# Two streamed value steps ahead of the second half of a softmax, and the home of the last four value tiles, in a two-layer decode kernel

## The chip, the core and the metric

The kernel runs on one core of one Trainium2 chip. The metric is device time in microseconds (us) of one execution. The engines are named as the profile names them: PE (TensorE, matrix multiply; PEld is its loading of weights), DVE (VectorE), ACT (ScalarE), POOL (GpSimd) and SP (SyncE, which here issues nearly all transfers, in its program's order). SBUF is the on-chip memory, PSUM the memory in eight banks that PE accumulates into, HBM the memory off the core.

## The reference

The work is one decode step (one token for each of four batch elements) through four blocks in a row: attention, feed-forward, attention, feed-forward, with the same weights and the same key and value caches in both attentions.

```python
x = A_x                                   # 4 x 1 x 512
for _ in range(2):
    h = layernorm(x)
    q = h @ wq                            # 32 query heads of 128, 8 key/value heads
    s = q . k_cache / sqrt(128)           # 4096 positions a head, 4 query heads share one
    x = x + (softmax(s) @ v_cache) @ wo
    h = layernorm(x)
    x = x + (gelu(h @ w_gate) * (h @ w_up)) @ w_down     # 1792 wide
```

All arrays are bf16. The keys and values of one element are 16.8 MB; the whole kernel reads 102.5 MB from HBM. Nearly all of it is keys and values, a part of the values twice.

## The kernel before, in words

**Tiles.** A cache tile is half of one head's keys or values: 128 partitions x 16 positions x 128, 512 KB. An element has 16 key tiles and 16 value tiles, in two groups of four heads (`one(b)` lists the value tiles as pairs of head and half, the first group's eight and then the second's). Keys are loaded to `KP`, which holds one element's 16 key tiles; values go through a ring of eight slots, `v_t`.

**Rounds.** The keys of an element are loaded once for both attentions. So the second attention of element b - 1 and the first attention of element b are worked together: `attend(b)` (L920) takes the scores of the second layer of b - 1 while its keys are still there, loads and turns the keys of b in the same places, takes the scores of the first layer of b, and goes through values of both. I call attend(1), attend(2), attend(3) rounds 1, 2 and 3. `attend_first` (L847) comes before them and `attend_last` (L1029) after them. Behind each attend stands `dense` (L1080), the feed-forward layer of element b, and the query projection of its second layer.

**What is kept.** Of the 16 value tiles of an element the second layer takes the last three from the ring (`kept`), two from PSUM, where DVE copied them (`Parked`, L500, and ACT copies them back, L507), and eleven from HBM again: three `own` and eight `other`, the first group's (`two`, L586).

**Two ways through a value tile.** `vals1` and `vals2` (class Values, L711) step through tiles in order. Most heads are done by 16 matmuls with the value tile as weights (L759, tile `ot`). A *streamed* head has the probabilities as weights instead: `stream_v` (L687) does eight matmuls of 128x256 for a tile (L692, tile `so`), and `turn_v` and `sum_v` (L698 to L709) fold the sums: a transpose, a reduction and a scaling on DVE. The eight `other` tiles are left behind by attend(b) as `late2`, a `Streamed` (L794), and worked in the dense layer, in its PE gaps: `fill` is one step, `whole` folds the sums of a pair of heads. They stand: one step after the residual sum (L1113), one in the middle of the gate matmuls (L1118), two behind the up matmuls (L1109), the first fold (L1122), two behind the down matmuls (L1129), and two in the second layer's query projection (L1229, L1242) with the last fold (L1257).

**What sets the order.** Everything is written out by hand, engine by engine; no scheduler moves it. PE, DVE and ACT each go through their instructions in order and wait where data are missing. All loads of keys and values are issued by SP in the order of the program. For values that is the order of `ring.seq`, to which `ring.extend` adds, and `ring.pump` issues as many loads as there are free slots. A load waits on SP for its slot to be read, and with it all that stand behind it; a load also waits for the eighth one before it to land, since there are eight semaphores in turn. `pump_head` loads both halves of a head in one transfer of 1 MB to a place outside the ring.

In `attend` the ring's order is: the first layer's value tiles of b (14 of them; two are loaded ahead), the eight `other` tiles, three `own` (L959 to L961). After these come two first-layer tiles of the next element (L1240) and its keys. The keys can be loaded once the second layer's scores have been taken.

**Around the softmax.** The last softmax of a round is at L1003. `soft` (L525) reduces, transposes and reduces on DVE (L530, L534, L535), scales (L539) and has ACT take the exponentials (L542). `soft_turn` transposes on DVE (L550), `soft_swap` (L563) has PE lay out the probabilities (L572, tile `x`) and ACT copies them back (L575); `soft_den` and `soft_recip` give the denominators. PE does three value steps of the other group (L1004) while DVE and ACT do the softmax. Behind it come the eight value tiles of the second group with the output projection between them, and the last head's output `OL_bf` (L605).

**The last element.** Its eight `other` tiles find no next element. The query weights of group gx (`wq_sb[gx]`, four tiles' worth) are free once the last projection with them is done, so four tiles go there (L1236). The other four go to the key tiles of the first scores (L1042 to L1044), which are free when those scores have been taken. `dense_last` (L1132) is the last feed-forward layer, for all four elements at once.

Of the kernel before, what the change touches and what calls it, by code (L numbers as in the profile page):

```python
# [8 lines left out]
FP32 = mybir.dt.float32  # L9
# [6 lines left out]
P = 128  # L16
# [9 lines left out]
GH = 4  # L26
# [8 lines left out]
def kernel(  # L35
# [21 lines left out]
    KD = D // P  # L57
# [736 lines left out]
    class Streamed:  # L794
# [3 lines left out]
            self.b, self.tiles, self.prob, self.dst, self.n = b, tiles, prob, dst, 0  # L798
            self.sums = []

        def fill(self):
            kvh, t = self.tiles[self.n]
            self.n += 1
            g, s = divmod(kvh, GH)
            pe = self.prob[g][0]
            if t == 0 and s % 2 == 0:
                ps = ps_sc.tile([P, 2 * SW], FP32, name="so", tag="sc")
                self.sums.append((kvh, ps))
            ps = self.sums[-1][1]
            ring.pump()  # L810
            v, own = ring.ready.pop((2, self.b, kvh, t))
            at = s % 2 * SW
            stream_v(ps[:, at:at + SW], pe[:, s], v, t, t == 0, t == NT - 1)
            assert own
            ring.free.append(v)
            ring.pump()

        def whole(self):
            kvh, ps = self.sums.pop(0)
            g, s = divmod(kvh, GH)  # L820
            turn_v(ps, 2)
            sum_v(ps, self.dst(kvh, 2), self.prob[g][1][:, s:s + 2], 2)

    def dst1(b):
        last = one(b)[-1][0]
# [94 lines left out]
    def attend(b, qy, before, norm, early=None):  # L920
# [35 lines left out]
        for t in range(NT):  # L956
            scores(sc2[1], gy, t)
            keys.load(GH)
        ring.extend(1, b, one(b)[ahead_of[b]:])  # L959
        ring.extend(2, b - 1, other2)  # L960
        ring.extend(2, b, own1)  # L961
        pe0, den0 = soft_swap(p0, early=True), soft_den(p0)

# [38 lines left out]
        scores(sc1, gy, 1)  # L1002
        p0 = soft(sc1)  # L1003
        vals1.step(3)  # L1004
        soft_turn(p0)
        heads = pairs(one(b))
        twice = o1(b)
        rows = RowProj(lambda i: twice(i).broadcast_to([P, 2]))
        prob1[gy] = (soft_swap(p0), soft_recip(soft_den(p0)))
        vals1.step(2)  # L1010
        rows.heads(heads[0], hp)
        vals1.step(2)
# [16 lines left out]
    def attend_last(q_bf, norm):  # L1029
        b = B - 1  # L1030
        gx, gy = second_groups[b]
        prob2 = {}
        kept2, own2, other2, apart2 = two(b)
        tiles = kept2 + own2 + apart2 + other2
        vals = Values(2, b, tiles, prob2, dst2(b),
                      streamed=[h for h in range(Hkv) if h != tiles[-1][0]],
                      paired=[h for h in range(Hkv) if h // 2 != tiles[-1][0] // 2])
        banks.back()
        sc2 = [new_scores(early=True)]
        scores(sc2[0], gx, 0)  # L1040
        qe = q_sums(q_bf[:])
        ring.pump_head(KP[gx][0][0][:])  # L1042
        ring.pump([k_tile(gx * GH + 2, 0)])
        ring.pump([k_tile(gx * GH + 3, 0)])  # L1044
        scores(sc2[0], gx, 1)
        q_spread(qe)
        p0 = soft(sc2[0], norm)
        rows = RowProj(o2)
        sc2.append(new_scores())
        scores(sc2[1], gy, 0)  # L1050
        scores(sc2[1], gy, 1)
        soft_turn(p0)
        pe0, den0 = soft_swap(p0), soft_den(p0)
        p1 = soft(sc2[1], norm, lasting=True)
        prob2[gx] = (pe0, soft_recip(den0))
        vals.step(8, hold=True)
        soft_turn(p1)
        vals.flush()
        pe1, den1 = soft_swap(p1), soft_den(p1)
        prob2[gy] = (pe1, soft_recip(den1))  # L1060
        heads = pairs(tiles)
        full = ps_x.tile([P, KF, WIDE], FP32, name="gr", tag="x")
        nothing(full.rearrange("p c r -> p (c r)"))
        nc.scalar.preload_act_table_set("gelu_apprx_tanh_and_others")
        vals.step(4)
        rows.heads(heads[0], hp)
        rows.heads(heads[1], hp)
        vals.step(2)
        rows.heads(heads[2], hp)
        rows.split()  # L1070
        vals.step(2)
        proj = OutProj(o2, B)
        proj.heads(heads[3], rep)
        rows.onto(proj)
        proj.n = Hq - rep
        proj.heads(heads[3] + rep, rep)
        assert vals.left() == 0 and ring.at == len(ring.seq)
        return proj.y, full

    def dense(b0, nb, y, prev, scr):  # L1080
# [34 lines left out]
        add_y(b0, nb, y)  # L1115
        rstd, mr = ln_scale(nb, st)
        t = [None if first else shifts(scr, mr, i) for i in range(2)]
        g = out_of(0, into(wg_sb, "g", prev.fill))  # L1118
        sq = gelu(scr, g, shifts(scr, mr, 0) if first else t[0], rstd, up)
        uv = out_of(1, u[0]) if first else u[0]  # L1120
        H_bf = gate_up(scr, sq, uv, shifts(scr, mr, 1) if first else t[1], rstd)
# [3 lines left out]
            busy(1)  # L1125
            return y
        y = down_rows(H_bf)
        for _ in range(2):
            prev.fill()  # L1129
        return turn_rows(y)  # L1130

    def dense_last(y, full):  # L1132
# [66 lines left out]
        for k in range(KD):  # L1199
            (nc.sync, nc.scalar)[k % 2].dma_start(out=rows_out[:, k * P:(k + 1) * P],  # L1200
                                                  in_=xo[k * QS:k * QS + B, :])

    class NoValues:
        fill = whole = lambda self: None

# [4 lines left out]
    for b in range(B):  # L1210
# [14 lines left out]
        if b:  # L1225
# [5 lines left out]
                rest = q_rows(b, gy)  # L1231
            norm.root()
            if b == B - 1:
                last = two(b)[2]
                ring.extend(2, b, last[:KD])
                for t in range(0, KD, NT):  # L1236
                    ring.pump_head(wq_sb[gx][:, t:t + NT].rearrange("p t (c d) -> p t c d", d=Dh))
            q_build(q_bf[:])
            if b < B - 1:
                ring.extend(1, b + 1, one(b + 1)[:ahead_of[b + 1]])  # L1240
# [1 line left out]
            prev.fill()  # L1242
            if b == B - 1:
                banks.back_brief()
                ring.extend(2, b, last[KD:])
                q_bf = q_tile()
                q_round(q_bf, turn_rows(rest), gy, norm)
        else:
# [51 lines left out]
```

## Time and profile before

| | us |
|---|---|
| median of three runs | 273.52 |
| the three runs | 272.98, 273.52, 275.62 |
| the profiled execution | 273.24 |
| its span in the profile | 271.46 |
| PE busy, DVE busy, ACT busy | 180.9, 176.3, 54.1 |
| transfers of keys and values: share of the span that 16 DMA engines were busy with the queue | 94.8% |
| matmuls on the last value tile begin; the output's transfers are issued | 261.90; 268.76 |

The profile is of one execution, so times out of it are set against its own 273.24 us; 1.78 us of that lie around the span. Times in the text are us from the start of the span. A line of the chain or of the timeline has the start, the length, the engine, the tile written and the line in the program, and `x16` for sixteen instructions together; in brackets stands how long the engine idled before and what ended that. "SPq" is SP's queue and "DMA v_t" a transfer to a value slot from its issue to its landing. In the page's slices, each column is a fortieth of the span; PEclk is the granted clock of PE in tenths, DMA the busy share of the 16 DMA engines in tenths.

### The profile page before, as it was taken

The page shows a single profiled execution, that of the slowest core. Times are in us where ns is not written, and L with a number is a line of the kernel's source. Part 1 is how long each engine was busy: PE and PEld are TensorE (multiplying, and loading weights), DVE is VectorE, ACT ScalarE, POOL GpSimd, SP SyncE. Part 2 cuts the span into 40 slices and gives each one's busy share as a digit, 9 for nine tenths or more (in the row PEclk, how much of TensorE's full clock was granted, in tenths as well). Part 3 has the DMA queues.
Part 4 walks back from the last instruction along what each step waited for, and adds up shares of the span by engine and source line. Part 5 has one row for each costly group of instructions (what it writes and reads, how often), then busy time and mean ns, then how long its engine had stood idle before and what let it go on. Part 6 is the DMA issues. An engine that isn't in the chain of part 4 may idle for free.

```text
span 271.5 us, 8960 instructions
## 1 busy us (share of the span) xinstructions
PE 180.9 (67%) x3982; PEld 110.6 (41%) x3982; DVE 176.3 (65%) x445; ACT 54.1 (20%) x113; POOL 2.7 (1%) x8
## 2 busy tenths in 40 slices
PE   1366254644696956868669458787596596977784
PEld 1313133533363524445327134454262253543463
DVE  3394951131224898875776989667759894877673
ACT  1001001100005402031023520310226102105630
POOL 2000000000000000000000000000000000000001
PEclk9999999555599795779997977799978556799999
DMA  7999999999984999999999999999999999999930
GB/s 250 422 416 421 416 421 416 410 383 406 407 325 147 405 415 419 418 418 416 416 404 407 417 420 417 417 416 388 381 421 418 416 423 414 369 383 378 415 132 3
DMA packets 32286, 103.08 MB, mean 380 GB/s; under 512 B 2676, under 2 KB 8568, under 8 KB 32248
## 3 DMA queue, kind: packets, MB, share of 16 engines
q1 hardware_dynamic: 32224, 102.51, 94.8%
q8 instruction: 31, 0.51, 0.7%
q14 instruction: 7, 0.06, 0.0%
q10 hardware_dynamic: 24, 0.01, 0.0%
HBM read 102.50 MB, written 0.00 MB: 378 GB/s over the span
## 4 chain that ended last, share of the span: by engine, by line
DMA 37%; DVE 28%; PE 23%; SPq 6%; issue 3%; ACT 1%; DVEq 0%
DMA v_t<-in_A_v_cache_dram 18%; DVE kp L488 16%; PE sc L521 10%; DMA kp<-in_A_k_cache_dram 9%; DMA wd_sb<-in_B_w_down_dram 6%; DMA kp<-in_A_v_cache_dram 4%; SPq L143 4%; PE ot L759 3%; PE so L692 2%; DVE pe L530 2%; DVE qb L313 2%; PE y L248 2%; PE q L273 1%; DVE q L280 1%; SPq L144 1%
## 5 line engine op out<-in xcount | busy, mean ns | idle before, releaser
L488 DVE STREAM_TRANSPOSE kp<-kp 128x1024 f32<-128x1024 f32 x64 | 74.1, 1208 | 0.0
L521 PE MATMUL sc<-kp,qb 128*32 128x512 bf16 x512 | 57.9, 492 | 20.7 <-DVE kp L488 15.2
L759 PE MATMUL ot<-pe,v_t 128*128 128x32 bf16 x1120 | 34.9, 182 | 13.0 <-DMA v_t<-in_A_v_cache_dram 11.6
L759 PEld LDWEIGHTS <-v_t 128*128 128x128 bf16 x1120 | 33.2, 101 | 23.8 <-DMA v_t<-in_A_v_cache_dram 13.8
L521 PEld LDWEIGHTS <-qb 128*32 128x32 bf16 x512 | 17.0, 106 | 48.6 <-issue 34.6
L542 ACT ACTIVATE pe<-sc,nl 128x512 bf16<-128x512 f32 x8 | 5.5, 687 | 88.8 <-DVE pe L539 61.8
L572 PE MATMUL x<-pe,ident_bf 128*32 128x128 bf16 x192 | 6.3, 262 | 16.5 <-DVE pe L550 16.5
L530 DVE TENSOR_REDUCE pe<-sc 128x1 f32<-128x512 f32 x12 | 8.3, 690 | 11.8 <-PE sc L521 11.8
L572 PEld LDWEIGHTS <-ident_bf 128*32 128x32 bf16 x256 | 5.9, 109 | 19.5 <-issue 18.2
L692 PE MATMUL so<-v_t,pl 128*32 128x256 bf16 x192 | 9.5, 275 | 3.6 <-DMA v_t<-in_A_v_cache_dram 3.4
L248 PE MATMUL y<-OT_bf,wo_sb 128*128 128x32 bf16 x192 | 7.3, 190 | 6.9 <-DMA wo_sb<-in_A_wo_dram 6.7
L248 PEld LDWEIGHTS <-wo_sb 128*128 128x128 bf16 x256 | 8.5, 102 | 8.1 <-DMA wo_sb<-in_A_wo_dram 7.1
L700 DVE STREAM_TRANSPOSE so<-so 128x256 f32<-128x256 f32 (+1 forms) x19 | 11.1, 583 | 1.0 <-PE so L692 0.9
L692 PE MATMUL so<-v_t,pe 128*32 128x256 bf16 x208 | 10.6, 338 | 1.2 <-ACT pe L575 1.1
L507 ACT COPY v_t<-park 128x1024 bf16<-128x1024 bf16 x12 | 11.3, 1031 | 0.0
L550 DVE STREAM_TRANSPOSE pe<-pe 128x512 bf16<-128x512 bf16 x12 | 8.4, 698 | 4.4 <-ACT pe L542 4.4
L370 DVE TENSOR_TENSOR xb<-XX,y 128x4 bf16<-128x4 f32 (+1 forms) x9 | 1.6, 174 | 14.5 <-PE y L248 14.4
L575 ACT CAST pe<-x 128x512 bf16<-128x512 f32 x12 | 7.0, 586 | 19.0 <-PE x L572 19.0
L605 DVE TENSOR_TENSOR OT_bf<-ot,rden 128x8 bf16<-128x8 f32 (+1 forms) x20 | 3.1, 157 | 10.7 <-PE ot L759 10.5
L351 PE MATMUL yr<-wo_sb,OT_bf 128*2 128x512 bf16 (+1 forms) x96 | 9.8, 478 | 0.1
L248 PE MATMUL q<-xb,wq_sb 128*128 128x5 bf16 (+1 forms) x192 | 5.5, 170 | 6.5 <-DMA wq_sb<-in_A_wq_dram 6.5
L307 PE MATMUL qe<-q_bf,ident_bf 128*32 128x16 bf16 x256 | 4.4, 176 | 8.0 <-DVE q_bf L296 6.1
(142 smaller groups left out, 217.3 us busy)
## 6 DMA issues: line engine op xcount, KB each, us to landing
v_t<-in_A_v_cache_dram SPq DMA_DIRECT2D x97, 512.0 KB, 8.4
kp<-in_A_k_cache_dram SPq DMA_DIRECT2D x40, 512.0 KB, 12.1
kp<-in_A_k_cache_dram SPq DMA_DIRECT2D x12, 1024.0 KB, 7.4
wq_sb<-in_A_wq_dram SPq DMA_DIRECT2D x2, 2048.0 KB, 14.7
wo_sb<-in_A_wo_dram SPq DMA_DIRECT2D x4, 1024.0 KB, 11.6
wq_sb<-in_A_v_cache_dram SPq DMA_DIRECT2D x2, 1024.0 KB, 10.8
wg_sb<-in_B_w_gate_dram SPq DMA_DIRECT2D x1, 1792.0 KB
wu_sb<-in_B_w_up_dram SPq DMA_DIRECT2D x1, 1792.0 KB
```

The source lines that it names most:

```text
L143: dq.dma_start(out=wo_sb[:, i * n:(i + 1) * n], in_=wo_dram[:, i * n:(i + 1) * n])
L248: nc.tensor.matmul(dst, lhsT=lhsT, rhs=rhs, start=first, stop=last, skip_group_check=True)
L351: nc.tensor.matmul(self.rows[j:j + x.shape[1]], lhsT=x, rhs=wo_sb[:, i], start=self.n < QD, stop=True, skip_group_check=True)
L488: nc.vector.transpose(out=words, in_=words)
L507: nc.scalar.copy(out=dst[:, i * n:(i + 1) * n], in_=self.parts[i])
L521: nc.tensor.matmul(sc[s * QS:(s + 1) * QS], lhsT=qb[:, w0:w0 + 2 * W], rhs=kt[:, :, be // 2, :, be % 2], start=(t == 0 and be == 0), stop= ...
L530: nc.vector.tensor_reduce(out=m, in_=sc.rearrange("p c j -> p (c j)"), axis=AX.X, op=ALU.min if norm else ALU.max)
L550: nc.vector.transpose(out=flat, in_=flat)
L572: nc.tensor.matmul(x[a * QS:(a + 1) * QS, s], lhsT=ident_bf[:, s * QS:(s + 1) * QS], rhs=pT[:, a], start=True, stop=True, skip_group_check ...
L692: nc.tensor.matmul(ps[d, :NW * QS], lhsT=x[:, w:w + NW].rearrange("p c h -> p (c h)"), rhs=v[:, i:i + NW, d], start=first and i == 0, stop ...
L700: nc.vector.transpose(out=flat, in_=flat)
L759: nc.tensor.matmul(self.ot[:, s % 2], lhsT=v[:, i, :], rhs=wide(pe[:, s, t * CH + i, :]), start=(done == 0 and i == 0), stop=(done == NT - ...
```

## The change

It has two parts.

*Steps into the softmax wait.* Two of the eight `other` steps, both halves of the first head, leave the dense layer and stand behind the three value steps in the wait for the round's last softmax. Their sums go to a bank of their own (`ps_h`) and are folded right behind the layout matmuls of that softmax. The second head of the group now stands alone too, in a tile of one head's width, and the third and fourth are folded as a pair. In the dense layer there is no step in the middle of the gate matmuls any more and one instead of two behind the down matmuls; so the six steps there are: one after the residual sum, two behind the up matmuls, one behind the down matmuls, two in the query projection. The first of the pair's four steps is the second of the two behind the up matmuls; it writes the one bank of `ps_sc` in which the second head's sums still lie, and PE waits there only for its own earlier matmuls. The ring's order follows: the two tiles are loaded between the first group's and the second group's first-layer tiles. No load is added or left out.

*The last four tiles.* All eight `other` tiles of the last element go to the query weights' space: four to group gx's as before, and four to group gy's, in one transfer of 1 MB and two of 512 KB, which wait for the second projection (L1231) to have read it. The loads to the key tiles in `attend_last` are gone.

```diff
@@ -798,28 +798,30 @@
             self.b, self.tiles, self.prob, self.dst, self.n = b, tiles, prob, dst, 0
             self.sums = []
 
-        def fill(self):
+        def fill(self, early=False):
             kvh, t = self.tiles[self.n]
             self.n += 1
             g, s = divmod(kvh, GH)
             pe = self.prob[g][0]
-            if t == 0 and s % 2 == 0:
-                ps = ps_sc.tile([P, 2 * SW], FP32, name="so", tag="sc")
-                self.sums.append((kvh, ps))
-            ps = self.sums[-1][1]
+            alone = s < 2
+            if t == 0 and (alone or s % 2 == 0):
+                pool, tag = (ps_h, "h") if early else (ps_sc, "sc")
+                n = 1 if alone else 2
+                self.sums.append((kvh, n, pool.tile([P, n * SW], FP32, name="so", tag=tag)))
+            ps = self.sums[-1][2]
             ring.pump()
             v, own = ring.ready.pop((2, self.b, kvh, t))
-            at = s % 2 * SW
+            at = 0 if alone else s % 2 * SW
             stream_v(ps[:, at:at + SW], pe[:, s], v, t, t == 0, t == NT - 1)
             assert own
             ring.free.append(v)
             ring.pump()
 
         def whole(self):
-            kvh, ps = self.sums.pop(0)
+            kvh, n, ps = self.sums.pop(0)
             g, s = divmod(kvh, GH)
-            turn_v(ps, 2)
-            sum_v(ps, self.dst(kvh, 2), self.prob[g][1][:, s:s + 2], 2)
+            turn_v(ps, n)
+            sum_v(ps, self.dst(kvh, n), self.prob[g][1][:, s:s + n], n)
 
     def dst1(b):
         last = one(b)[-1][0]
@@ -956,8 +958,10 @@
         for t in range(NT):
             scores(sc2[1], gy, t)
             keys.load(GH)
-        ring.extend(1, b, one(b)[ahead_of[b]:])
-        ring.extend(2, b - 1, other2)
+        ring.extend(1, b, one(b)[ahead_of[b]:TG])
+        ring.extend(2, b - 1, other2[:NT])
+        ring.extend(1, b, one(b)[TG:])
+        ring.extend(2, b - 1, other2[NT:])
         ring.extend(2, b, own1)
         pe0, den0 = soft_swap(p0, early=True), soft_den(p0)
 
@@ -1002,11 +1006,15 @@
         scores(sc1, gy, 1)
         p0 = soft(sc1)
         vals1.step(3)
+        for _ in range(NT):
+            late2.fill(early=True)
         soft_turn(p0)
         heads = pairs(one(b))
         twice = o1(b)
         rows = RowProj(lambda i: twice(i).broadcast_to([P, 2]))
-        prob1[gy] = (soft_swap(p0), soft_recip(soft_den(p0)))
+        swapped, den = soft_swap(p0), soft_den(p0)
+        late2.whole()
+        prob1[gy] = (swapped, soft_recip(den))
         vals1.step(2)
         rows.heads(heads[0], hp)
         vals1.step(2)
@@ -1039,9 +1047,6 @@
         sc2 = [new_scores(early=True)]
         scores(sc2[0], gx, 0)
         qe = q_sums(q_bf[:])
-        ring.pump_head(KP[gx][0][0][:])
-        ring.pump([k_tile(gx * GH + 2, 0)])
-        ring.pump([k_tile(gx * GH + 3, 0)])
         scores(sc2[0], gx, 1)
         q_spread(qe)
         p0 = soft(sc2[0], norm)
@@ -1115,7 +1120,7 @@
         add_y(b0, nb, y)
         rstd, mr = ln_scale(nb, st)
         t = [None if first else shifts(scr, mr, i) for i in range(2)]
-        g = out_of(0, into(wg_sb, "g", prev.fill))
+        g = out_of(0, into(wg_sb, "g", None))
         sq = gelu(scr, g, shifts(scr, mr, 0) if first else t[0], rstd, up)
         uv = out_of(1, u[0]) if first else u[0]
         H_bf = gate_up(scr, sq, uv, shifts(scr, mr, 1) if first else t[1], rstd)
@@ -1125,8 +1130,7 @@
             busy(1)
             return y
         y = down_rows(H_bf)
-        for _ in range(2):
-            prev.fill()
+        prev.fill()
         return turn_rows(y)
 
     def dense_last(y, full):
@@ -1200,6 +1204,9 @@
             (nc.sync, nc.scalar)[k % 2].dma_start(out=rows_out[:, k * P:(k + 1) * P],
                                                   in_=xo[k * QS:k * QS + B, :])
 
+    def in_wq(g, t, n):
+        return wq_sb[g][:, t:t + n].rearrange("p t (c d) -> p t c d", d=Dh)
+
     class NoValues:
         fill = whole = lambda self: None
 
@@ -1231,10 +1238,12 @@
                 rest = q_rows(b, gy)
             norm.root()
             if b == B - 1:
-                last = two(b)[2]
-                ring.extend(2, b, last[:KD])
-                for t in range(0, KD, NT):
-                    ring.pump_head(wq_sb[gx][:, t:t + NT].rearrange("p t (c d) -> p t c d", d=Dh))
+                ring.extend(2, b, two(b)[2])
+                ring.pump_head(in_wq(gx, 0, NT))
+                ring.pump_head(in_wq(gx, NT, NT))
+                ring.pump_head(in_wq(gy, 0, NT))
+                for t in range(NT, KD):
+                    ring.pump([in_wq(gy, t, 1)[:, 0]])
             q_build(q_bf[:])
             if b < B - 1:
                 ring.extend(1, b + 1, one(b + 1)[:ahead_of[b + 1]])
@@ -1242,7 +1251,6 @@
             prev.fill()
             if b == B - 1:
                 banks.back_brief()
-                ring.extend(2, b, last[KD:])
                 q_bf = q_tile()
                 q_round(q_bf, turn_rows(rest), gy, norm)
         else:
```

## Prediction

> **What bounds the kernel now.** I read the page's slices first, then the chain of work that ended last in order of time, then the timeline of the third round (the pass that finishes element 2 and begins element 3), then the last four microseconds, then the DMA queue.
>
> ```profile
> PEclk9999999555599795779997977799978556799999
> DMA  7999999999984999999999999999999999999930
> GB/s 250 422 416 421 416 421 416 410 383 406 407 325 147 405 415 419 418 418 416 416 404 407 417 420 417 417 416 388 381 421 418 416 423 414 369 383 378 415 132 3
> ```
>
> A slice is 6.8 us. Away from the start, the end and one hole at 75 to 88 us, the DMA engines move 370 to 420 GB/s: a 512 KB tile takes 1.23 us at full rate (landing marks 120.60, 121.84 and 123.05 us). So transfers are a bound; the chain tells where they are the bound.
>
> ```profile
> 117.05 8.49 DMA v_t<-in_A_v_cache_dram
> 125.59 0.58 PE ot L759 x16
> 126.19 0.19 DVE OL_bf L605
> ...
> 136.43 2.10 PE sc L521 x26
> ...
> 171.61 8.86 DMA v_t<-in_A_v_cache_dram
> 180.51 0.58 PE ot L759 x16
> 181.12 0.19 DVE OL_bf L605
> ...
> 182.27 6.15 DMA v_t<-in_A_v_cache_dram
> ...
> 191.70 2.05 PE sc L521 x30
> ...
> 226.76 0.70 DVE pe L530
> ...
> 237.41 0.19 DVE OL_bf L605
> ...
> 238.57 6.23 DMA v_t<-in_A_v_cache_dram
> ...
> 250.39 11.46 DMA kp<-in_A_v_cache_dram
> ```
>
> Each round runs from one OL_bf (the last head's output, after which the dense layer may start) to the next: 126.19, 181.12, 237.41, so 54.93 and 56.29 us. Rounds 1 and 2 end on a value tile that was queued 8.5 and 8.9 us behind others; round 3 has no transfer between 191.70 and 237.41, so DVE and PE set it. From the softmax's first reduction (L530) to OL_bf takes 10.65 us in round 3 (226.76 to 237.41), against 11.10 in round 1 (its L530 starts at 115.09) and 10.91 in round 2 (170.21). Compute alone would thus have ended only 0.45 and 0.26 us sooner: both bounds lie almost upon each other. That decides this forecast.
>
> ```profile
> 226.65 1.46 PE L759 MATMUL ot<-pe,v_t 128*128 128x32 bf16 x48
> ...
> 229.89 0.41 PE L572 MATMUL x<-pe,ident_bf 128*32 128x128 bf16 x16 [1.78 <-DVE pe L550]
> ...
> 230.66 0.26 DVE L560 RECIPROCAL rden<-den 128x16 f32<-128x16 f32 x1 [0.82 <-PE den L555]
> ...
> 261.90 0.57 PE L759 MATMUL ot<-pl,kp 128*128 128x32 bf16 x16 [0.41 <-DMA kp<-in_A_v_cache_dram]
> ...
> 262.71 0.28 PE L248 MATMUL y<-masks,yt 128*128 128x32 bf16 x4
> ```
>
> Here is the softmax wait: PE idles 1.78 us, DVE 0.82 us. The last two lines are the end: the last tile is waited for 0.41 us, but yt (DVE L358, 261.66 + 0.75 = 262.41) is nearly as late.
>
> **The change part by part.** The sum is made against the profiled execution: 273.24 us, span 271.46, so 1.78 us lie around the span; the median shown is 273.52.
>
> Two streamed steps in the wait. A step is 8 matmuls of `so`, 0.40 us (244.84, 0.40, x8); two are 0.80 us in a PE gap of 1.78, so nothing, if both tiles are there. They now stand in queue places 9 and 10 of the round's values; those places landed at about 116.6 and 117.8 in round 1, where the swap (L572) starts at 118.22, and 1.5 us or more ahead of need in round 3. If the gap is gone: +0.8 a round. The matching sum (transpose 0.47, reduce 0.19, scaling 0.16, rows L700 to L708 at 235.39) is 0.82 us of DVE, put where DVE idles 0.82: nothing, at worst +0.82. A gain is excluded for both, since nothing on that path was removed.
>
> The order of transfers. Two second-layer tiles are now ahead of the last eight first-layer tiles of a round. In round 1, where the tile queue is the bound, the last of these lands 2 x 1.23 = 2.45 us later: +2.45. The slots don't prevent it: places 17 and 18 are freed by the early steps at some 117 and 118 us, when the tile before is still 7 us from landing; on SP, in order, the next loads (behind the parked tiles, 120.44 and 121.63 us) stand behind these two and are not yet due. In round 2 the whole stream again has its two extra tiles, but its start is the same, so its last tile is again 2.45 later than before; not a further 2.45. Compute, also 2.4 late and 0.26 ahead of the queue, agrees. In round 3 the values have slack (tile landed 235.85, used 236.82), and the shift rides on compute.
>
> The dense stage has six steps instead of eight, and the last tiles that it waits for land two tiles earlier after OL_bf. OL_bf to first scores is 10.24, 10.58 and 10.74 us at the three passes; the second and third hold waits for tiles (0.44 us at 188.47, 0.58 us at 244.84), the first has none on its chain but 0.67 us of steps at 132.77, of which the transpose of y hides all but about 0.05. I take 10.2 for the first two and 10.3 for the third, where PE still has the second projection: -0.05, -0.36, -0.45. No loss here, nothing is added.
>
> The second pair's first step writes the bank in which the second head's sums lie, without a wait for DVE: no cost.
>
> Key loads. They follow the scores, which are now later against the stream: after the last first-layer tile 11 tiles (13.5 us) are queued instead of 13 (16 us), and the first key pair is issued some 11.4 us after OL_bf (192.80 - 181.12 = 11.68). The margin falls from 5 us to about 2. On an empty queue the row is: pair issued 84.19, then 16, 119 and 348 GB/s in the next three stretches of 1 us, about 1.8 us lost. The last two prefetch tiles wait for steps 7 and 8, so about 0.5 us may be lost at each boundary; but the stream had 1 to 1.5 us of dips there (347 GB/s in 188 to 191), which the earlier tiles fill. Bounds: -1 to +1.8 for the stream; I take 0, as keys land about as before (144.4) while their turns (L488) start 2.4 later. The Trainium skill, DMA: Bandwidth & Descriptors, Specifications, gives a first-byte latency of about 0.6 us for this kind of queue; by it there would be no gap, and the sum would be the same; the row above is slower than that, and I go by the row.
>
> The last four tiles go to the second query weights' space. They can be issued when that projection has read it, at about +10.1 us after OL_bf, where before the last was issued at 250.39. At 249.27 the pair issued at 246.15 was still 7.7 us from landing (256.93), so the stream was full anyway: 0, between -0.5 and 0. SP has nothing behind these but the output. If that cover is gone (the chain later, the queue drained), the earlier issue is worth up to 2 us, which the rivals hold.
>
> The end. With the stream about 2 us ahead of compute there, the waits at 260.92 and 261.90 go; next is yt at 262.41 instead of PE's 262.71: -0.26 (the row gives 0.30; 0.04 is PE's issue).
>
> Sum: 2.45 - 0.05 - 0.36 - 0.45 - 0.26 = +1.33, so 273.24 + 1.33 = 274.6 us, half a per cent over the profile.
>
> **The rivals.** (a) The stream sets the end and the chain follows it. For it: it is the bound of rounds 1 and 2, and deeper queues remove dips. Against 418 GB/s the stretches 188 to 194 lose 0.77 us and 232 to 251 lose 1.99 (384, 330, 389, 386, 397, 355 GB/s): 273.24 - 2.76 = 270.5. Against: round 3 shows no transfer on its path.
>
> (b) The clock. The granted clock moves in pieces of 3.41 us; after each softmax wait it is 0.50 (232 to 234 us, 174 to 176), and sixteen `so` matmuls take 1.08 us there instead of 0.62 at 1.0. Two steps in the wait may keep it at 1.0: of 6.4 us from swap to OL_bf about 1 us goes in round 3, where alone it counts: 274.6 - 1.0 = 273.6. Against: 1 us of idle PE remains. The Trainium skill, TensorE: Matmul & The Clock Gate, Part 1, says that a free-running window of about 3.4 us of PE activity sets the clock; the pieces agree, the threshold is not shown by this case. The clock also gives round 3 its 35.06 us from scores to softmax against 33.78 in round 2: chance of +/-1.3.
>
> (c) The key loads run dry. From the point where the last prefetch tile has landed before the pair's data starts (margin under 1.8 us), each of two boundaries costs up to 1.8, and the next round's last tile is as much later: 274.6 + 1.8 = 276.4 with one in full, 278.2 with both. For it: margin worked out at 2, with one or two transfers in flight only. Against: 1 us of slack of keys before their turn.
>
> (d) It doesn't do what it says: the two tiles come too late for the wait and hold up the swap. Round 1 has 0.4 us to spare, rounds 2 and 3 more: 274.6 + 0.8 = 275.4.
>
> **How the numbers follow.** Forecast 0.44, (a) 0.12, (b) 0.17, (c) 0.20, (d) 0.07. The time is the forecast's, 274.6. The range leaves out most of (a) and the worse half of (c): 272.2 (forecast with 1.0 for the clock and 1.3 for its phase) to 276.8. A measurement of this kernel tells about 1% from no change: 2.7 us, so 270.8 and 276.3 on 273.5. Faster: two thirds of (a), 0.08. Slower: (c) with most of its cases and a little of the forecast's tail, 0.22. Same: 0.70.
>
> **What would show it.** Right: the last value tile of round 1 lands near 128.0 and OL_bf near 128.6; the `so` pair with 128x256 sits between the x48 and L572, whose start moves no further than its L530; no wait for transfers in the dense stage; the last tile lands at about 260, before PE asks for it. Wrong: OL_bf of round 1 at 126 (the order costs nothing); transfers at 0 to 150 GB/s near 140 and 196 us (rival c); clock 1.0 behind the softmax (b); an end on the last tile (a).

## The result, and the profile after

| | median us (runs) | profiled execution | its span | mean granted clock |
|---|---|---|---|---|
| before | 273.83 (272.98 to 275.62) | 273.24 | 271.46 | 0.843 |
| after | 284.88 (283.58 to 287.91) | 283.58 | 281.80 | 0.809 |

The changed kernel takes 1.038 times as long (95% interval 1.030 to 1.045). The forecast was 274.6, range 272.2 to 276.8: it is 10.3 us too low. Of one kernel below, `fold_wait_alone`, three of the four executions were disturbed (280.6 to 283.6 us at a clock of 0.80 to 0.81, against 276.2 us at 0.85), so it has no ratio and its repetition carries the reading.

The slices of the page of the profile after:

```profile
PEclk9999999555698995759999558677697757978998
DMA  7999999999949999999899999997899999988930
GB/s 253 420 417 420 418 421 416 397 386 417 395 161 347 417 419 418 416 417 416 286 340 419 416 420 416 417 417 240 285 416 416 417 418 417 418 342 254 377 126 3
```

There are three new holes of two slices each: 286 and 340 (134 to 148 us), 240 and 285 (190 to 204), 342 and 254 (247 to 261). Each lies behind an OL_bf, in the dense layer. A slice is 7.05 us here; measured against 418 GB/s the holes cost some 3.5, 5.2 and 4.0 us of transfers. In the kernel before, the slices at the same places (404 and 407, 388 and 381, 369, 383 and 378) cost 0.4, 1.1 and 2.0.

The marks of the rounds, from the timelines of DVE and PE (us; "dense" is OL_bf to the first scores behind it):

| | OL_bf of round 1 | round 2 | round 3 | last OL_bf to the end | dense, three times |
|---|---|---|---|---|---|
| before | 126.19 | 54.93 | 56.29 | 34.05 | 10.24, 10.58, 10.74 |
| after | 128.34 | 58.53 | 58.96 | 35.97 | 10.98, 12.43, 12.94 |

These marks are of one profiled execution of each kernel. The 10.3 us between the two spans are 2.15 in round 1, 3.60 in round 2, 2.67 in round 3 and 1.92 behind it. The chain of waits shows two things that were not in the forecast:

```profile
118.28 9.41 DMA v_t<-in_A_v_cache_dram
127.74 0.58 PE ot L759 x16
...
134.22 0.20 DVE ov L707
134.47 0.40 PE so L692 x8
134.87 0.81 PE y L273 x56
...
176.71 9.50 DMA v_t<-in_A_v_cache_dram
...
236.53 8.65 DMA v_t<-in_A_v_cache_dram
```

First, the fold of the second head (L700 to L707) and the step behind it (L692) now stand on the chain, between the layer's hidden values and its down matmuls (y L273): from 133.81 to 134.87 that is 1.06 us. PE's timeline shows the wait in round 2. Before, PE goes to the down matmuls as soon as the hidden values (L433) are there:

```profile
186.72 0.97 PE L273 MATMUL y<-wd_sb,words 128*32 128x128 bf16 x56 [0.30 <-DVE words L433]
```

After, it waits for the fold (L707) and does the step first:

```profile
193.59 0.40 PE L692 MATMUL so<-v_t,pl 128*32 128x256 bf16 x8 [1.95 <-DVE ov L707]
193.81 0.95 PE L273 MATMUL y<-wd_sb,words 128*32 128x128 bf16 x56
```

Secondly, all three rounds now end on a value tile, round 3 too, which before had no transfer on its path.

How the transfers fall dry is seen in SP's queue. The timeline of SP behind the OL_bf of round 2, first before (OL_bf 181.12), then after (OL_bf 186.87); the columns are start, length, place, tiles and how many loads stand together:

```profile
182.27 9.48 SPq L623 DMA_DIRECT2D v_t<-in_A_v_cache_dram  x8
192.80 2.83 SPq L481 DMA_DIRECT2D kp<-in_A_k_cache_dram  x4
```

And the same view after:

```profile
188.02 11.54 SPq L623 DMA_DIRECT2D v_t<-in_A_v_cache_dram  x6
201.22 2.54 SPq L481 DMA_DIRECT2D kp<-in_A_k_cache_dram  x4
```

Before, eight loads go out in 9.5 us: each streamed step gives its slot back, and that slot's load is the next in line. After, six go out in 11.5 us. At 0.524 MB each that is 272 GB/s of new loads. The keys, which wait for the scores, come 14.35 us behind OL_bf instead of 11.68. The windows of the profile (columns: stretch, its length, busy time and instructions of PE, PEld, DVE, ACT and POOL, clock, DMA share, GB/s), before:

```profile
186.00:192.00 6.00, 4.29 (x140) 2.49 (x143) 4.28 (x19) 0.41 (x2) 0.00 (x0) 1.00 1.00 373
192.00:199.00 7.00, 4.84 (x88) 2.25 (x84) 4.23 (x12) 1.18 (x3) 0.00 (x0) 0.90 1.01 400
```

The windows after:

```profile
191.00:197.00 6.00, 3.62 (x100) 1.74 (x92) 3.08 (x13) 0.21 (x1) 0.00 (x0) 0.78 0.69 227
197.00:204.00 7.00, 5.76 (x88) 2.21 (x84) 4.39 (x17) 0.41 (x2) 0.00 (x0) 0.67 0.85 274
```

The DMA engines are idle for 31 and 15% of the two stretches after, and the clock is at 0.78 and 0.67 where it was at 1.00 and 0.90. Bytes issued by SP less bytes moved give the tiles in flight; at 0, 2, 4, 5, 6, 8, 10 and 12 us behind this OL_bf they are 3.2, 2.5, 2.1, 2.2, 2.5, 2.1, 2.8 and 2.4 before, and 2.8, 2.2, 0.7, 0.2, 1.0, 1.0, 1.1 and 1.2 after.

### The profile page after: what moved, and what is told of

Its sections match the earlier page's. It is cut to its first block, busy times and chain, and to the rows that moved or that the text cites. A ratio compares the mean times of both kernels' runs of the same rounds, so it can differ in the third digit from the quotient of the medians.

```text
span 281.8 us, 8963 instructions
## 1 busy us (share of the span) xinstructions
PE 186.3 (66%) x3978; PEld 111.3 (40%) x3982; DVE 177.8 (63%) x454; ACT 54.1 (19%) x113; POOL 2.7 (1%) x8
## 4 chain that ended last, share of the span: by engine, by line
DMA 43%; PE 25%; DVE 21%; SPq 5%; issue 2%; ACT 2%; DVEq 0%; ACTq 0%
DMA v_t<-in_A_v_cache_dram 27%; DMA kp<-in_A_k_cache_dram 11%; DVE kp L488 8%; PE sc L521 7%; DMA wu_sb<-in_B_w_up_dram 5%; PE ot L759 4%; SPq L143 4%; PE so L692 3%; PE q L273 2%; DVE pe L530 1%; PE y L248 1%; DVE qb L313 1%; DVE q L280 1%; PE g L273 1%; PE u L248 1%
## 5 line engine op out<-in xcount | busy, mean ns | idle before, releaser
L759 PE MATMUL ot<-pe,v_t 128*128 128x32 bf16 x1120 | 35.5, 183 | 14.2 <-DMA v_t<-in_A_v_cache_dram 11.5
L692 PE MATMUL so<-v_t,pl 128*32 128x256 bf16 x192 | 10.6, 306 | 9.9 <-DVE ov L707 7.2
L530 DVE TENSOR_REDUCE pe<-sc 128x1 f32<-128x512 f32 x12 | 8.3, 690 | 13.2 <-PE sc L521 13.2
L700 DVE STREAM_TRANSPOSE so<-so 128x256 f32<-128x256 f32 (+1 forms) x22 | 11.6, 529 | 7.1 <-PE so L692 7.0
L692 PE MATMUL so<-v_t,pe 128*32 128x256 bf16 x208 | 11.3, 327 | 5.9 <-DMA v_t<-in_A_v_cache_dram 3.7
L572 PE MATMUL x<-pe,ident_bf 128*32 128x128 bf16 x192 | 6.2, 247 | 12.2 <-DVE pe L550 12.2
L572 PEld LDWEIGHTS <-ident_bf 128*32 128x32 bf16 x256 | 5.9, 103 | 14.4 <-issue 13.3
L351 PE MATMUL yr<-wo_sb,OT_bf 128*2 128x512 bf16 (+1 forms) x96 | 10.7, 505 | 0.0
L692 PEld LDWEIGHTS <-pl 128*32 128x32 bf16 x240 | 5.3, 101 | 13.1 <-DVE ov L707 8.2
L692 PEld LDWEIGHTS <-pe 128*32 128x32 bf16 x208 | 5.3, 102 | 12.8 <-issue 6.5
L605 DVE TENSOR_TENSOR OT_bf<-ot,rden 128x8 bf16<-128x8 f32 (+1 forms) x20 | 3.1, 156 | 11.2 <-PE ot L759 11.2
## 6 DMA issues: line engine op xcount, KB each, us to landing
wq_sb<-in_A_v_cache_dram SPq DMA_DIRECT2D x3, 1024.0 KB, 10.3
```

Source lines behind the costliest of these rows:

```text
L351: nc.tensor.matmul(self.rows[j:j + x.shape[1]], lhsT=x, rhs=wo_sb[:, i], start=self.n < QD, stop=True, skip_group_check=True)
L530: nc.vector.tensor_reduce(out=m, in_=sc.rearrange("p c j -> p (c j)"), axis=AX.X, op=ALU.min if norm else ALU.max)
L572: nc.tensor.matmul(x[a * QS:(a + 1) * QS, s], lhsT=ident_bf[:, s * QS:(s + 1) * QS], rhs=pT[:, a], start=True, stop=True, skip_group_check ...
L692: nc.tensor.matmul(ps[d, :NW * QS], lhsT=x[:, w:w + NW].rearrange("p c h -> p (c h)"), rhs=v[:, i:i + NW, d], start=first and i == 0, stop ...
L700: nc.vector.transpose(out=flat, in_=flat)
L759: nc.tensor.matmul(self.ot[:, s % 2], lhsT=v[:, i, :], rhs=wide(pe[:, s, t * CH + i, :]), start=(done == 0 and i == 0), stop=(done == NT - ...
```

## The experiments

The expectations set two theories against each other. *Shallow queue*: with two steps gone from the dense layer and two tiles fewer behind the last first-layer tile, too few loads are allowed out there. *Fold wait*: the step that writes into the second head's bank waits for its fold on DVE, and holds up PE and the slots behind it.

**The order alone.** `order_alone` is the kernel before with only the ring's new order; all eight steps stay in the dense layer. `order_one` brings one tile forward instead of two.

```diff
-        ring.extend(1, b, one(b)[ahead_of[b]:])
-        ring.extend(2, b - 1, other2)
+        ring.extend(1, b, one(b)[ahead_of[b]:TG])
+        ring.extend(2, b - 1, other2[:NT])     # order_one: other2[:1]
+        ring.extend(1, b, one(b)[TG:])
+        ring.extend(2, b - 1, other2[NT:])     # order_one: other2[1:]
```

> The kernel before with the ring's new order alone: two second-layer tiles are loaded ahead of the last eight first-layer tiles, but all eight steps stay in the dense layer where they were. Fold wait theory (the loss is PE's wait for the second head's fold): no such wait is here, so the order costs what the prediction gave it, 2.5 us in round 1 and little after, 275 to 277 us. Shallow queue theory (the loss is that two tiles fewer are queued behind the last first-layer tile): as much as the change or more, 282 to 288 us, with 200 to 300 GB/s in the stretches of 12 us behind each dense layer's start. All the work of the reference is done.

> The kernel before with one second-layer tile instead of two ahead of the last eight first-layer tiles; steps where they were. Shallow queue theory: about half of what two cost (8.9 us), 276.5 to 279.5 us, or less if the old depth had a margin. If the cost of the order were only the last tile's delay, 1.23 us: 275.0 us. All the work of the reference is done.

Measured: 282.73 us, ratio 1.033 [1.025, 1.040], and 278.78 us, ratio 1.022 [1.019, 1.025]. PE waits for that fold in neither; one tile costs 2.2%, two cost 3.3%. In `order_alone` OL_bf of round 1 comes 2.2 us later, as in the changed kernel, but rounds 2 and 3 take 57.75 and 58.54 us with the dense stage at 10.2 to 10.9: the loss lies in the transfers. Only 1.2 tiles are in flight at the OL_bf of round 2, since two slots hold the two early tiles until their steps. The chain at the end of this round shows what that does:

```profile
177.14 2.46 DVE park L500 x4
179.60 0.02 SPq L623
179.62 0.04 issue
179.66 5.81 DMA v_t<-in_A_v_cache_dram
185.47 0.04 issue
185.51 0.61 PE ot L759 x16
186.13 0.02 issue
186.15 0.18 DVE OL_bf L605
```

The last first-layer tile gets no slot until DVE has parked another tile, at 179.60, and OL_bf waits for it. In the changed kernel, whose early steps have given their slots back by then, this load goes out at 176.71 and stands 9.50 us in a full queue. So `order_alone` shows that the ring is short of slots, but in part at another place than the changed kernel; what stands nearest to the change is the next pair of runs.

**Without the fold's wait.** In `no_fold_wait` the second and third heads are the pair and the fourth stands alone; the fold goes behind the layer's last sum. `steps_sooner` also puts a step back into the gate matmuls and takes the last one out of the projection.

```diff
-            alone = s < 2
+            alone = s in (0, GH - 1)
...
-        prev.whole()
         if first:
             y = down(nb, H_bf)
...
         add_y(b, 1, y)
+        prev.whole()
```

> The changed kernel, but the second and third head are the pair and the fourth stands alone, folded where the queries' matmuls run: no step of the dense layer waits for a fold; all steps stay where the change put them. Fold wait theory: the gain is most of the loss, 274 to 277 us, and transfers at over 390 GB/s behind the dense layer. Shallow queue theory: PE's wait of 2 us goes, but the steps behind the down matmuls and the projection free their slots as late as before, so 281 to 284 us, with the dips still there.

> The changed kernel with the second and third head as the pair (no fold wait), and the six steps of the dense layer as early as the tiles come: one behind the residual sum, one in the middle of the gate matmuls, two behind the up matmuls, one behind the down matmuls, one in the projection. Same order of transfers, same 11 tiles behind the last first-layer tile, but three slots are free 1 to 2 us sooner and the last one 1.1 us sooner. Shallow queue theory: a third to two thirds of the 8 us that are left without the fold wait come back, 276 to 279.5 us. If the order alone sets the cost, as without the fold wait: 281 to 283 us. All the work of the reference is done.

Measured: 281.82 us, 1.027 [1.020, 1.035], and 279.94 us, 1.025 [1.019, 1.030]. The second lies between its two expectations. The queue still runs low in the first: 2.1, 2.5, 2.1, 0.6 and 0.5 tiles are in flight at 2, 4, 5, 7 and 9 us behind the OL_bf of round 2. So the wait is not the greater part, and spreading the steps better gains nothing that the intervals can tell.

**The last four tiles.** `last_four` is the kernel before with part 2 of the change alone, `early_steps` the changed kernel with part 2 undone.

> The kernel before with the second part alone: the last four value tiles go to the second query weights' space. Both theories, fold wait and shallow queue, leave this part out of the loss: the queue is 7.7 us deep when the earlier load is issued, so 273.2 to 273.9 us, within 0.3% of before. Above 276 us it would carry a part of the 11 us itself.

> The changed kernel with its second part undone. Both theories: the whole loss is still here, 284 to 286 us. If the last four tiles are worth something once the queue is shallow at the end (they are issued at 257.7 to 260.0 us there, before the scores are done), it is up to 1.5 us slower than the changed kernel, 286.4 us.

Measured: 273.47 us, 0.997 [0.993, 1.000], and 287.90 us, 1.050 [1.043, 1.056]. Part 2 changes nothing that can be told in the kernel before. In the changed one its absence goes with 3.0 us more (287.90 - 284.88), twice what was expected, but that is not shown to be its doing: the two programs differ only behind the last OL_bf, and there the profiles take as long, 35.92 us in `early_steps` and 35.97 in the changed kernel. The difference lies ahead of it (OL_bf at 250.18 instead of 245.83), where both do the same; the clock was lower in that execution (0.782, 0.809 in the other). Why is open, and it is a warning that a gap of 3 us between two such kernels can have another cause than the edit.

**The fold's wait alone.** The kernel before, with one of the two steps behind the down matmuls moved ahead of them, where it waits for the fold. Order and number of the loads stay.

```diff
-                for _ in range(2):
+                for _ in range(3):
                     prev.fill()
...
-        for _ in range(2):
-            prev.fill()
+        prev.fill()
```

> The kernel before, old order and all eight steps in the dense layer, but the fifth step stands ahead of the down matmuls instead of behind them, so PE waits there for the first pair's fold as it does in the changed kernel for the second head's. Fold wait theory: about 1 us on the chain in each of three dense layers, and slots freed later, 278 to 284 us. Shallow queue theory: 1 us a dense layer at most, and less where the queue is deep, 274.5 to 277 us, with no stretch of the dense layer under 340 GB/s. All the work of the reference is done.

> The kernel before with its fifth step of the dense stage moved ahead of the last matmuls of the layer, where it waits for the second head's fold, run once more in more rounds, since the first time its runs lay between 276 and 284 us. Order of the tiles and number of steps are those of before. Shallow queue alone: 274.5 to 277. The fold's wait as a cost of its own size: 278 to 282.

Measured: 276.2 us in the first, and 277.3 us, a ratio of 1.012 [1.007, 1.018] (about +3.4 us), in the second. That is at the upper end of what the shallow queue alone allowed (277) and under what the wait as a cost of its own size was given (278): the wait costs something, but this run alone doesn't tell by which way. Its dense stage takes 11.47, 12.60 and 13.48 us against 10.24, 10.58 and 10.74.

**How many tiles the full rate needs.** `flight` leaves the layers out: it loads 24 tiles each through a ring of 1, 2, 3, 4, 5, 6 and 8 slots, and one matmul per tile gives the slot back. It ran once.

> No attention and no feed-forward: 24 value tiles each with 1, 2, 3, 4, 5, 6 and 8 slots, each slot freed by one matmul on its landing; the output is a copy of x. It measures what rate so many tiles in flight give. Shallow queue theory: a tile by itself takes some 4 us from issue to landing, so 1 gives 110 to 130 GB/s, 2 about 230, 3 about 330, and 4 or 5 are needed for 410. What the prediction took (a transfer needs 1.8 us of others ahead of it, then the rate is full): 1 gives 150 to 170, 2 gives 320 to 350, 3 and more give 415.

| slots | 1 | 2 | 3 | 4 | 5 | 6 | 8 |
|---|---|---|---|---|---|---|---|
| us from load to load | 3.58 | 2.17 | 1.68 | 1.40 | 1.28 | 1.28 | 1.28 |
| GB/s | 146 | 242 | 312 | 374 | 410 | 409 | 410 |

The times are means from the fifth load on.

The slices of its page show the same as a staircase:

```profile
GB/s 136 135 138 140 172 159 135 135 135 163 161 225 242 225 265 216 261 262 221 288 312 299 320 317 367 406 394 357 404 411 409 409 403 412 410 410 410 410 411 289
```

With one slot a tile comes round in 3.58 us, though its bytes need 1.28; the other 2.30 us are issue, notice of the landing and the matmul. Of the two expectations, the shallow queue's four or five slots for the full rate came true (its 110 to 130 GB/s for one slot was too low), and the prediction's three did not: three give 312 GB/s, four 374 and five 410. The Trainium skill, SBUF — State Buffer, The DMA setup-cost knee, says that each transfer pays some 2 us whatever its size, mostly between its last byte and its notice. The 2.30 us agree. In a ring of slots this part counts in full, since a slot is only given on behind the notice; the prediction's own row, the 1.8 us lost on an empty queue, held no return of a slot. What this does not explain is the count of five: a fixed 2.30 us beside 1.28 of bytes would be covered by three slots (3.58 / 1.28 = 2.8). The trace shows what is missing in that sum: a load takes longer when others are on their way, 3.2 us from issue to landing with one slot, 4.0 with two and 4.7 with three. Why it does stays open.

**Two more slots.** To make room for more than eight slots, the `half` kernels go without half of a weight: the output projection's weights are those of 16 heads, each used twice (that part of the computation is changed, the work on the engines is not), which frees 2 MB of loads at the start and room for ten slots. `half_before` is the kernel before, `half_nofold` is `no_fold_wait`, `half_after` the changed kernel; 8 and 10 are the slots.

```diff
-V_SLOTS = 8
+V_SLOTS = 10
...
-    wo_sb = wts.tile([P, Hq, D], BF16, name="wo_sb")
+    wo_sb = wts.tile([P, Hq // 2, D], BF16, name="wo_sb")
```

> The kernel before with the output weights of 16 heads only, each used for two heads (so the attention's output projection is changed; the amount of work on every engine is not), which loads 2 MB less at the start and leaves room for more ring slots. 8 slots as before. It is the base line of the three beside it. 2 MB are some 5 us of transfers at the 418 GB/s of the full stretches, in a first round that the stream bounds: 267 to 270 us by both theories.

> The base line (half of the output weights) with 10 ring slots instead of 8. In the kernel before, 2 to 3 tiles are in flight behind the last first-layer tile, with dips of 1 to 1.5 us a boundary. Shallow queue: two more tiles in flight fill these dips in rounds that the compute bounds as much: 0 to 2 us less than with 8 slots. Theory of the fold's wait: slots matter nothing, within 1 us of it.

> The changed kernel without the wait for the fold (the fourth head folded alone), with half of the output weights and 8 slots. Both theories: as far above its base line as the same kernel with all output weights was above the kernel before (2.7%): 6 to 9 us above half_before8, with 0.3 to 1.5 tiles in flight at 5 to 11 us behind OL_bf and 230 to 300 GB/s there.

> The same with 10 ring slots: the order of the transfers and of the steps is that of half_nofold8, only two more tiles may be on their way. Shallow queue: this gives back what the two moved steps no longer release in the dense stage, so 2 to 3 tiles in flight and 370 to 418 GB/s behind OL_bf, and the time returns to 0 to 3 us above half_before8 (the later last first-layer tile of round 1, 2.45 us, stays). Rival, that the order of the tiles or the later steps themselves hold up the dense stage: it stays within 2 us of half_nofold8.

> The changed kernel whole, with half of the output weights (each used for two heads: that part of the computation is changed) and 8 ring slots; its base lines are half_before8 (267.6 us) and half_nofold8 (276.0 us, the same without the wait for the fold). The step behind the second head's fold waits up to 3 us for DVE, and its slot and the later ones come free as much later. By the difference of the two full kernels (284.9 and 281.8) it is 2 to 4 us above half_nofold8, 278 to 280, by both theories.

> The same with 10 slots; half_nofold10 was at 272.0 us. If the fold's wait costs by freeing slots late (shallow queue), two more tiles on their way cover most of it: 0 to 1.5 us above half_nofold10, 272 to 273.5. If it costs by itself, through the time that PE stands idle and the lower clock behind it, it costs as much as with 8 slots: 2 to 4 us above, 274 to 276.

| | median us | ratio to the kernel before | OL_bf of round 1 | round 2 | round 3 | dense, three times |
|---|---|---|---|---|---|---|
| half_before8 | 267.61 | 0.978 [0.969, 0.988] | 120.53 | 55.52 | 54.82 | 10.37, 10.17, 10.38 |
| half_before10 | 266.90 | 0.975 [0.967, 0.982] | 120.99 | 55.11 | 55.18 | 10.50, 10.24, 10.30 |
| half_nofold8 | 276.04 | 1.009 [1.005, 1.012] | 123.64 | 59.12 | 58.18 | 10.86, 10.83, 10.82 |
| half_nofold10 | 272.01 | 0.994 [0.991, 0.998] | 122.96 | 56.25 | 56.42 | 10.66, 10.81, 11.40 |
| half_after8 | 280.38 | 1.027 [1.022, 1.031] | 123.05 | 58.54 | 60.58 | 12.02, 12.77, 12.28 |
| half_after10 | 276.80 | 1.013 [1.008, 1.017] | 123.09 | 58.79 | 58.62 | 12.43, 12.85, 12.90 |

The same stretch of the dense stage of round 2, 5 to 12 us behind OL_bf, in the windows of half_nofold8:

```profile
188.00:195.00 7.00, 4.66 (x144) 2.64 (x148) 5.05 (x21) 0.41 (x2) 0.00 (x0) 1.00 0.89 301
```

And in those of half_nofold10:

```profile
184.00:191.00 7.00, 4.38 (x144) 2.35 (x140) 5.41 (x23) 0.41 (x2) 0.00 (x0) 1.00 0.98 393
```

Same order, same steps, two more slots: 301 GB/s become 393, and 4.0 of the 8.4 us come back, where the kernel before gains 0.7 from them. What is left over half_before8 is 4.4 us, over the 3 that the shallow queue allowed: 2.4 of it is round 1, and behind rounds 1 and 2 the tiles in flight still fall to 0.6 or 0.7 and then 0.2 at 11 and 12 us behind OL_bf, just before the keys. Behind the last first-layer tile there are eleven loads and no longer thirteen, whatever the slots are. Nor are the ten slots ever all on their way: a load waits for the eighth one before it to land, and with ten slots SP spends 41.1 us in 45 such waits on value tiles (15.6 us in 14 with eight).

The fold's wait costs 4.3 us with 8 slots (280.38 - 276.04) and 4.8 with 10, more than the 2 to 4 that either expectation had; by the ratios to the kernel before it is 1.8% both times. So two more slots do not cover it, and it costs by itself. PE's timeline at the down matmuls behind round 3, of half_nofold10 (OL_bf at 235.63):

```profile
241.16 1.24 PE L273 MATMUL y<-wd_sb,words 128*32 128x128 bf16 x56 [1.98 <-DVE words L433]
```

And of half_after10 (OL_bf at 240.50):

```profile
247.24 0.61 PE L692 MATMUL so<-v_t,pl 128*32 128x256 bf16 x8 [2.47 <-DVE ov L707]
247.64 1.71 PE L273 MATMUL y<-wd_sb,words 128*32 128x128 bf16 x56
```

Without the wait the down matmuls begin with the hidden values (L433), 5.53 us behind OL_bf, and DVE folds later, behind the layer's last sum. With it they begin at 7.14. Of these 1.61 us the fold and the step make 1.05; the hidden values themselves are 0.61 later there, where the granted clock was 0.53 in the first 3.5 us behind OL_bf and 1.00 without the wait. The down matmuls then take 1.71 us instead of 1.24. With 8 slots the hidden values are the sooner ones in the kernel with the wait: 5.48 us behind OL_bf in half_after8 each time, 6.04 to 6.13 in half_nofold8. All the same its scores are later, behind fold, step and a clock of 0.50, 0.50 and 0.51 from 6 to 9 us, where half_nofold8 has 1.00 three times. The dense stage is 1.2 to 2.0 us longer in the kernels with the wait, and the keys wait for its scores.

## Why the prediction was wrong, step by step

**The order in round 1: right.** 2.45 us were forecast; OL_bf is 2.15 later, 2.21 with the order alone, 1.05 with one tile.

**"Not a further 2.45" in round 2: true only of a full stream.** With ten slots and no fold wait round 2 is 0.73 us longer than in half_before8; with eight it is 3.60.

**The steps in the wait and their fold at no cost: nearly right.** PE's timeline of round 3 after:

```profile
235.42 0.79 PE L692 MATMUL so<-v_t,pl 128*32 128x256 bf16 x16
237.26 0.41 PE L572 MATMUL x<-pe,ident_bf 128*32 128x128 bf16 x16 [1.05 <-DVE pe L550]
```

The pair takes 0.79 us out of the gap, and 1.05 are left. From the softmax's first reduction (L530) to L572 it is 3.13 us in rounds 1 and 3, as before; in round 2 the second step waits 0.84 us for its tile and it is 3.38. That is rival (d), at a quarter of a microsecond, in a round that ends on a tile anyway. Where the steps go was not the price; what they leave behind was.

**The key loads: the term that was mis-sized.** It stood at 0, between -1 and +1.8. The holes behind rounds 1 and 2 measured 3.5 and 5.2 us of transfers, 3.1 and 4.1 more than before. Its working took "11 tiles (13.5 us) are queued" as if they would follow one another at the full rate. Of the eleven, five were issued when the last first-layer tile landed in round 2 (186.21), and six were not: SP can issue only into a free slot, and these go out one for each step. Besides, the eleven counts landings, which come behind the bytes: at OL_bf five loads had yet to land, but only 2.8 tiles of bytes had yet to move. So the stream had 2.8 + 6 = 8.8 tiles left, 10.8 us at 1.23: less than the 11.4 us that the prediction gave the keys, and far less than the 14.35 that they took. Before it was 3.2 + 8 = 11.2 tiles, 13.8 us, for 11.68: a margin of 2 us and not of 5. The steps bunch besides: none gives a slot back between 187.57 and 191.06, and the next comes at 193.59. Rival (c) had the place and the sign, 0.20 of the chance, and a price of 276.4 to 278.2 that used one cold start instead of the count of slots.

**"Without a wait for DVE: no cost": wrong.** The description of the change says it too, that PE waits there only for its own matmuls. The step overwrites sums that DVE has yet to read, so it waits for the fold: fold and step are 1.06 us on the chain at each boundary. Alone it costs 3.4 us [1.9, 4.8], in the half kernels 4.3 and 4.8.

**The dense stage -0.05, -0.36, -0.45: wrong in sign.** (By its own choice of 10.2, 10.2 and 10.3 the terms are -0.04, -0.38 and -0.44; the sum is the same.) It is 0.74, 1.85 and 2.20 longer. The waits for tiles did go, but that did not matter beside the fold's wait and the clock.

**The last four tiles at 0: right alone** (0.997). What they are worth with the queue drained is not shown: the end behind the last OL_bf is 35.92 us without them and 35.97 with them.

**The end, -0.26:** right in size: from the scores behind the last OL_bf to the end of the span it is 23.03 us, 23.31 before, and the waits for the last tile are gone. That part 2 did it is not shown, since `early_steps` has 23.10.

**The clock (rival b)** came as that rival said at its place, and brought nothing: behind the softmax wait of round 3 it is 1.00 from 236 to 244 us, where it was 0.50 at 232 to 234 before, but the round now ends on a transfer. Over the whole it fell to 0.809 from 0.843; the dense layers are among the places (0.78 and 0.67 above).

No kernel that does all the work beat the one before: `last_four` comes nearest, with an interval that ends at 1.000. Of the 3.8%, the kernel without the fold's wait keeps 2.7 and the fold's wait alone makes 1.2, together 3.9; the intervals are some 0.5 to 0.8% wide to each side. What stays open is how the 2.7 divide between the order and the steps that moved, since the order alone (3.3%) loses its time in part elsewhere, and why ten slots give back only half of it.

## What to carry to other kernels

In a ring of slots a step that reads a tile is also the permit for a later load. When steps are moved, count the tiles in flight and the permits per microsecond in the stage that they leave, and not only the time in the stage that they enter. A list of loads in program order is no queue: only what has a free slot is on its way. And when a sum gets a bank to itself or loses one, ask of the next writer of that bank who still reads it; where that reader sits on another engine, the writer waits, with all that stands behind it.

## What the runs showed of the hardware

512 KB tiles through a slot ring from one queue run at 146, 242, 312, 374 and 410 GB/s with 1 to 5 slots, and no faster with 6 or 8 (one execution). The ring's eight slots are fewer than they look, as landed tiles hold theirs until their step: 2.8 tiles were in flight at the OL_bf of round 2, and 0.2 five microseconds later. And the two bounds that lay 0.3 to 0.5 us apart before made each loss count: what the dense layer's compute loses also delays the keys (11.68 us behind OL_bf became 14.35), and with them the next round's stream.
